# Attention and MLP in one kernel: batches pipelined in a manual order, heads in pairs, 64-key streaming blocks, wide exp and transposes

## The chip, the cores and the metric

The kernel runs on one core of one Trainium2 chip. The metric is device time in microseconds (us), the median of several executions. The executions of one kernel lie 0.1 to 1.5% apart, so I call differences under 2 us of the whole time nothing. Where a change is smaller, I read it from the stages of the profile. Times within a profile are counted from the start of its span, and the span is some 2 us shorter than the measured time.

## The reference

Four batches, 768 tokens, 8 heads of 64. Heads 0, 2 and 6 ("retrieval") have causal attention. The other five ("streaming") see only the first 4 keys (the sinks) and the last 64. The result, 512 wide, goes through an MLP that mixes tokens (768x768, twice) and channels (512x512, twice).

```
scores = q @ k.T / 8;  mask: causal, or causal & (key < 4 or query - key < 64)
x      = softmax(scores) @ v            -> [4, 768, 512]
theta  = x @ w_theta                     # "phases"
zr, zi = x * cos(theta), x * sin(theta)
y      = w_tok_r @ zr + w_tok_i @ zi     # "mixing", over tokens
u      = x + y
out    = u + relu(u @ w_ch)
```

## The kernel before

It is written in program order, attention of all four batches, then the MLP, and a scheduler orders the instructions. The parts that matter here:

```python
# attention, per batch and pair of neighbouring heads, per block of 128 tokens
nc.sync.dma_start(out=tmp..., in_=src[sl])                 # 64 KB
nc.gpsimd.tensor_copy(tmpb, tmp)                           # cast to bf16
nc.tensor.transpose(pt, tmpb, ident)                       # one 128x128
(nc.vector.tensor_copy if si == 0 else nc.scalar.copy)(dst[:, sl], pt)
# ... per head and block j of 128 keys, at most 512 queries
nc.tensor.matmul(ps[:, :cn], kT[:, j*128:(j+1)*128], qT[...], start=True, stop=True)
nc.scalar.activation(at[...], ps[:, :cn], AF.Exp, scale=scale)
# ... per block of queries: mask, then values (65 columns: v and a column of ones)
nc.vector.tensor_tensor(blk, blk, m, ALU.mult)
nc.tensor.matmul(av[i], blk, vt[:, j, :], start=(n == 0), ...)
# ... normalization, per head and block
nc.vector.reciprocal(r, av[i][:, D:D+1])
nc.scalar.activation(xe, av[i][:, :D], AF.Copy, scale=r)
nc.vector.tensor_copy(x_sb[b][i][:, h*D:(h+1)*D], xe)
# [cut] then transposes of x, the token weights (loaded and transposed), and per batch:
# phases (4 matmuls, two sines, two products on DVE), mixing (12 matmuls, add, 4 transposes),
# channels (4 matmuls, relu on ACT, add on DVE, store)
```

The softmax here doesn't subtract the row's maximum and nothing guards it: scores larger than these inputs give would overflow.

## Time and profile before

| | before |
|---|---|
| median | 379.77 us (378.25 to 380.51, 4 runs) |
| span of the profiled run | 377.8 us |
| one batch of attention | 48 us |
| one batch of MLP | 29.4 us (mixing 22.6, phases 6.8) |
| transposes of x, between attention's end and the first mixing | 205 to 246 us |

The prediction shows the lines. Its first fence has busy time by engine and then the span in 40 slices, a digit being tenths of a slice. A timeline row has start, duration, engine, source line, operation, output and inputs, shape and count, and in brackets how long the engine was idle before and what ended that. A matmul's *duration* is modelled and holds its latency, so the cost of a matmul in a stream is the distance from its start to the next one's.

### The profile page before, as it was taken

Reading aid. Unit: us, or ns where it says so; the run is one execution under the profiler, and the core shown is the slowest. Engines: PE = TensorE matmul, PEld = TensorE weight load, DVE = VectorE, ACT = ScalarE, POOL = GpSimd, SP = SyncE. Lnnn points to the kernel's source line nnn. Section 1 sums busy time; section 2 is a strip of 40 time slices with the busy share of each in tenths; the row PEclk is TensorE's granted clock in tenths of the full one; section 3 lists DMA queues with packets and bytes.
Section 4 is the critical chain, followed back from the end, with each engine's and each line's share of the span. In section 5 each row is a group of like instructions: output and inputs, shape, how many; then the busy total and the mean of one; then the engine's idle time right before and its main releaser. Section 6 shows DMA issues by size and latency. Waiting matters only on the chain.

```text
span 377.8 us, 6882 instructions
## 1 busy us (share of the span) xinstructions
PE 313.4 (83%) x1709; PEld 141.5 (37%) x1724; DVE 241.0 (64%) x1243; ACT 197.1 (52%) x598; POOL 97.2 (26%) x406
## 2 busy tenths in 40 slices
PE   0178897889878899789897985687998998999994
PEld 0033443334333434334343443343553443443442
DVE  1126674666756667666576679666788558658655
ACT  1048787877778778777787673000037018008103
POOL 7156545444454445544441000000000000000000
PEclk9999999999999999999999988576999999999999
DMA  6955445444443444434440000034022004004004
GB/s 185 261 129 121 107 92 113 100 95 95 97 100 87 102 110 99 95 88 104 108 102 1 2 0 1 0 90 162 1 84 86 2 0 167 2 1 167 2 0 167
DMA packets 84616, 31.39 MB, mean 83 GB/s; under 512 B 78944, under 2 KB 79968, under 8 KB 84576
## 3 DMA queue, kind: packets, MB, share of 16 engines
q1 hardware_dynamic: 83520, 29.91, 30.3%
q0 software_dynamic: 1056, 1.05, 1.7%
q8 instruction: 13, 0.21, 0.2%
q14 instruction: 27, 0.22, 0.2%
HBM read 25.69 MB, written 6.29 MB: 85 GB/s over the span
## 4 chain that ended last, share of the span: by engine, by line
PE 60%; DVE 14%; ACT 14%; issue 5%; DMA 4%; SPq 1%; POOL 0%; ACTq 0%; POOLq 0%; DVEq 0%
PE ps L136 16%; PE py L215 8%; PE py L212 8%; PE avt L152 8%; ACT at L138 7%; PE pc L225 4%; PE pth L198 4%; PE pt L103 4%; DVE at L151 4%; ACT xe L158 4%; PE pt L165 3%; DVE xT L166 2%; DVE x L159 2%; DMA tmp<-in_q_dram 2%; PE pt L220 2%
## 5 line engine op out<-in xcount | busy, mean ns | idle before, releaser
L138 ACT ACTIVATE at<-ps 128x256 bf16<-128x256 f32 (+3 forms) x236 | 95.4, 420 | 31.8 <-PE avt L152 14.8
L136 PE MATMUL ps<-qT,kT 64*128 64x256 bf16 (+3 forms) x236 | 92.7, 424 | 11.6 <-ACT at L138 5.5
L101 POOL CAST tmpb<-tmp 128x128 bf16<-128x128 f32 x192 | 56.9, 305 | 95.2 <-PE pt L103 27.1
L152 PE MATMUL avt<-vt,at 128*128 128x65 bf16 x552 | 65.1, 243 | 12.3 <-DVE at L151 9.0
L228 ACT ACTIVATE rl<-pc 128x512 f32<-128x512 f32 x24 | 14.3, 597 | 108.5 <-PE pc L225 108.5
L158 ACT ACTIVATE xe<-avt,r 128x64 bf16<-128x64 f32 x192 | 58.4, 313 | 13.5 <-DVE r L156 12.5
L103 PE MATMUL pt<-ident,tmpb 128*128 128x128 bf16 x192 | 49.5, 288 | 19.2 <-POOL tmpb L101 11.6
L152 PEld LDWEIGHTS <-at 128*128 128x128 bf16 x552 | 39.9, 120 | 54.7 <-DVE at L151 41.4
L159 DVE COPY x<-xe 128x64 bf16<-128x64 bf16 x192 | 37.8, 198 | 17.7 <-ACT xe L158 17.1
L103 PEld LDWEIGHTS <-tmpb 128*128 128x128 bf16 x192 | 20.0, 116 | 59.0 <-POOL tmpb L101 31.0
L212 PE MATMUL py<-zr,wrT 128*128 128x512 bf16 x141 | 39.8, 392 | 1.0 <-ACT ct L203 0.8
L215 PE MATMUL py<-zi,wiT 128*128 128x512 bf16 x140 | 39.4, 392 | 0.1
L104 DVE COPY qT<-pt 128x128 bf16<-128x128 bf16 x96 | 20.7, 216 | 25.8 <-PE pt L103 22.2
L156 DVE RECIPROCAL r<-avt 128x1 f32<-128x1 f32 x192 | 28.9, 157 | 11.4 <-PE avt L152 11.4
L104 ACT COPY kT<-pt 128x128 bf16<-128x128 bf16 x96 | 25.3, 265 | 19.7 <-PE pt L103 19.0
L136 PEld LDWEIGHTS <-kT 64*128 64x128 bf16 x236 | 20.8, 103 | 25.6 <-issue 9.2
L198 PE MATMUL pth<-w_theta_sb,xT 128*128 128x512 bf16 x92 | 27.3, 414 | 2.4 <-ACT ct L203 1.6
L151 DVE TENSOR_TENSOR at<-at,m_causal 128x128 bf16<-128x128 bf16 x72 | 16.6, 239 | 17.0 <-ACT at L138 16.4
L165 PE MATMUL pt<-ident,x 128*128 128x128 bf16 x96 | 19.0, 260 | 8.6 <-DVE xT L166 8.4
L217 DVE TENSOR_TENSOR u<-x,py 128x512 bf16<-128x512 bf16 x24 | 16.5, 687 | 14.5 <-PE py L215 13.6
L107 POOL CAST vt<-tmpv 128x64 bf16<-128x64 f32 x96 | 23.4, 244 | 8.9 <-DMA tmpv<-in_v_dram 7.9
L221 DVE COPY uT<-pt 128x128 bf16<-128x128 bf16 x96 | 18.8, 221 | 10.4 <-PE pt L220 9.4
(51 smaller groups left out, 345.8 us busy)
## 6 DMA issues: line engine op xcount, KB each, us to landing
tmp<-in_q_dram SPq DMA_DIRECT2D x96, 64.0 KB, 2.1
tmp<-in_k_dram SPq DMA_DIRECT2D x96, 64.0 KB, 2.1
tmpv<-in_v_dram SPq DMA_DIRECT2D x96, 64.0 KB, 2.2
out_dram<-ot SPq DMA_DIRECT2D x24, 256.0 KB, 2.0
tmp<-in_moe_w_tok_r_dram SPq DMA_DIRECT2D x6, 384.0 KB, 4.4
tmp<-in_moe_w_tok_i_dram SPq DMA_DIRECT2D x6, 384.0 KB, 3.4
w_theta_sb<-in_moe_w_theta_dram POOLq DMA_DIRECT2D x1, 512.0 KB, 6.0
w_ch_sb<-in_moe_w_ch_dram POOLq DMA_DIRECT2D x1, 512.0 KB, 10.1
```

Source lines behind the costliest of these rows:

```text
L101: nc.gpsimd.tensor_copy(tmpb, tmp)
L103: nc.tensor.transpose(pt, tmpb, ident)
L104: (nc.vector.tensor_copy if si == 0 else nc.scalar.copy)(dst[:, sl], pt)
L136: nc.tensor.matmul(ps[:, :cn], kT[:, j * 128:(j + 1) * 128], qT[:, sq0 + off: sq0 + off + cn], start=True, stop=True)
L138: nc.scalar.activation(at[:, sq0 + off:sq0 + off + cn], ps[:, :cn], AF.Exp, scale=scale)
L151: nc.vector.tensor_tensor(blk, blk, m, ALU.mult)
L152: nc.tensor.matmul(av[i], blk, vt[:, j, :], start=(n == 0), stop=(n == len(js) - 1), skip_group_check=True)
L158: nc.scalar.activation(xe, av[i][:, :D], AF.Copy, scale=r)
L159: nc.vector.tensor_copy(x_sb[b][i][:, h * D:(h + 1) * D], xe)
L198: nc.tensor.matmul(pth, xT_sb[b][kk][:, i * 128:(i + 1) * 128], w_theta_sb[:, kk, :], start=(kk == 0), stop=(kk == KD - 1))
L212: nc.tensor.matmul(py, wrT[s][:, t * 128:(t + 1) * 128], zr[s], start=(s == 0), stop=False)
L215: nc.tensor.matmul(py, wiT[s][:, t * 128:(t + 1) * 128], zi[s], start=False, stop=(s == NB - 1))
```

## The change

Its intent: put attention of batch b+1 under the MLP of batch b, in an order fixed by hand, and give each engine fewer and wider instructions. Cut to its core:

```diff
+    ctx.enter_context(tc.manual_schedule())
+PAIRS = [(0, 2), (4, 6), (1, 3), (5, 7)]          # two heads, one in each row half
+            for pair in range(max(map(len, mms))):  # scores: the two heads in turn
+                for y in range(2):
+                        nc.tensor.matmul(o, l, r, start=True, stop=True, ...)
+                # streaming heads: 64 keys against 128 queries, output in a column half
+                            half = slice(64 * (c % 2), 64 * (c % 2) + 64)
+                            mms[y].append((ps[half, y, ...], kT[n][rows, c*64:(c+1)*64], qT[n][rows, lo:hi]))
-                    nc.scalar.activation(at[...], ps[:, :cn], AF.Exp, scale=scale)
+                nc.scalar.activation(P[:, :, :w0], ps[:, :, :w0], AF.Exp, scale=scale)   # two banks
+        # six transposes into one bank, one copy of 768 columns
+                for j in range(NB):
+                    nc.tensor.transpose(pt[:, j*128:(j+1)*128], src[:, j], ident)
+                    nc.scalar.copy(dst[n], pt[:, :S])
+        # normalization of four heads at once, on DVE alone
+            nc.vector.reciprocal(r, av[:, :, D])
+            nc.vector.tensor_tensor(dst, av[:, :, :D], r.unsqueeze(2).to_broadcast([128, 4, D]), ALU.mult)
+            nc.gpsimd.tensor_tensor(zi[:, i], x[:, i], st, ALU.mult)                     # was DVE
+            nc.vector.scalar_tensor_tensor(ot, pc, 0.0, u[:, t], ALU.max, ALU.add)       # relu and add
+    drain(transposes(0)); drain(scores(0)); drain(values(0)); drain(token_weights())
+    for b in range(B):
+        if b + 1 < B:
+            for n in range(4):
+                cast(b + 1, n)
+            weave((phases(b), 5184), (transposes(b + 1), 2720))
+            fetch(b + 1)
+            weave((mix(b), 23000), (chain(scores(b + 1), values(b + 1)), 14000))
+        else:
+            drain(phases(b))
+            drain(mix(b))
```

`weave` advances its parts in proportion to their estimated cost. [Cut: the masks, the sink keys of all streaming heads scored by one set of matmuls, a copy of v shifted by 64 tokens for the half-width value matmuls, and the token weights cast by the transfer itself.]

## The prediction

> **What bounds the kernel now.** I read the page first (busy shares, then slices), then the windows view to split the span, then the chain, the timeline of TensorE, and the groups by shape.
>
> ```profile
> PE 313.4 (83%) x1709; PEld 141.5 (37%) x1724; DVE 241.0 (64%) x1243; ACT 197.1 (52%) x598; POOL 97.2 (26%) x406
> ...
> PE   0178897889878899789897985687998998999994
> PEld 0033443334333434334343443343553443443442
> DVE  1126674666756667666576679666788558658655
> ACT  1048787877778778777787673000037018008103
> POOL 7156545444454445544441000000000000000000
> ```
>
> The reader is to see two programs in a row. ACT and POOL work in the first 22 slices (attention) and almost nothing after (MLP), so adding the stages up engine by engine wastes each engine for half of the time. The windows view puts numbers on it:
>
> ```profile
> core 0: us, PE busy (x) PEld busy (x) DVE busy (x) ACT busy (x) POOL busy (x), PEclk, DMA share, GB/s
> 25.00:205.00 180.00, 156.39 (x914) 68.76 (x913) 117.51 (x809) 140.70 (x486) 85.55 (x356) 1.00 0.43 98
> 205.00:283.00 78.00, 64.80 (x350) 32.85 (x356) 56.82 (x269) 19.84 (x47) 0.00 (x0) 0.82 0.12 39
> 283.00:377.80 94.80, 86.33 (x427) 37.90 (x435) 62.47 (x149) 31.78 (x56) 0.00 (x0) 1.00 0.16 60
> ```
>
> In the attention stage TensorE counts as busy 87% of the time, but its 914 matmuls would fit in far less. The timeline shows why:
>
> ```profile
> 42.43 0.39 PE L136 MATMUL ps<-qT,kT 64*128 64x256 bf16 x1
> 42.76 0.35 PE L152 MATMUL avt<-vt,at 128*128 128x65 bf16 x3
> 43.04 0.39 PE L136 MATMUL ps<-qT,kT 64*128 64x256 bf16 x1
> 43.36 0.29 PE L103 MATMUL pt<-ident,tmpb 128*128 128x128 bf16 x1
> 43.59 0.28 PE L136 MATMUL ps<-qT,kT 64*128 64x128 bf16 x1
> ```
>
> A 64-row score matmul of 256 columns starts at 42.43 and the 128-row one behind it at 42.76: 330 ns later. In the MLP 512 columns take 216 ns start to start, so 256 should take 107. The switch of shape costs some 0.15 to 0.22 us, and the scheduler mixes shapes freely. So the attention stage is bound by many small instructions, with waits passed between TensorE, ACT and DVE. The MLP is bound by matmuls and, between batches, by ACT's sines:
>
> ```profile
> 343.54 0.88 PE pth L198 x4
> 344.44 0.60 ACT st L202
> 345.66 1.04 PE pth L198 x4
> 347.22 0.69 ACT ct L203
> 347.95 1.04 PE pth L198 x4
> ```
>
> From the first matmuls of py and pth in the timeline, one MLP batch takes 29.4 us (320.8 to 350.2): 22.6 of mixing and 6.8 of phases. One attention batch takes 48 us (the last x copies of batches 0, 1, 2 end at 75.8, 123.7, 171.8).
>
> **What the Trainium skill says.** "TensorEngine Tiling (Array Packing)", Key Properties, says that a change of tiling mode drains TensorE; the 330 ns above agree. "ScalarE: Activation LUTs", What ACT_TABLE_LOAD costs, gives 1283 ns for the load; this trace has two, 1283 ns each. "VectorE: DVE Perf Modes", the perf-mode tier table, gives tensor_tensor two elements a cycle in bf16 from SBUF and one from PSUM or in fp32; the trace agrees: a 128x128 bf16 mask is 218 to 239 ns, a 128x512 with PSUM or fp32 684 to 692. "GPSIMD Engine Reference", the comparison of a tensor_tensor on GPSIMD with DVE, has 4497 ns at 2048 fp32 elements. The kernel before has no such operation on POOL; my estimate from that page is 1.2 us for 512 elements.
>
> **The change part by part.** Durations for new sizes are fits to rows of the groups by shape:
>
> ```profile
> L138 ACT ACTIVATE at<-ps 128x256 bf16<-128x256 f32 x124 | 46.3, 384 | 8.0 <-PE ps L136 4.4
> L138 ACT ACTIVATE at<-ps 128x512 bf16<-128x512 f32 x56 | 33.4, 597 | 22.1 <-PE avt L152 14.8 <-PE ps L136 6.4
> L158 ACT ACTIVATE xe<-avt,r 128x64 bf16<-128x64 f32 x192 | 58.4, 313 | 13.5 <-DVE r L156 12.5
> L159 DVE COPY x<-xe 128x64 bf16<-128x64 bf16 x192 | 37.8, 198 | 17.7 <-ACT xe L158 17.1
> ```
>
> An exp grows by 213 ns for 256 columns, 0.83 a column on 171: 1.03 us for 1024. A PSUM copy of 128 columns is 221; at 0.52 ns a column 512 are 0.42 and 768 are 0.55 on DVE (0.8 on ACT).
>
> 1. *Removed:* 236 exps become 56 of mostly 1024 columns; per batch 9 x 1.03 + 3 x 0.6 + 0.92 + 0.39 + 0.7 = 13.1 us against 24.4. All 192 ACT scalings (58.4 us) and 192 DVE copies (37.8) go; 48 wide DVE multiplies of some 0.43 and 48 reciprocals of 0.16 take their place. The 24 ACT relus go into one DVE operation. 372 masks become 72.
>
> 2. *Moved:* the built order on TensorE shows a long start for batch 0, three periods (phases of batch b with transposes of b+1, then mixing of b with scores and values of b+1), and an end with phases and mixing of batch 3.
>
> 3. *The mixing stage, per period, TensorE:* 96 matmuls x 0.216 = 20.7; 48 transposes x 0.056 = 2.7; retrieval scores, two heads in the two row halves at once, 2688 columns / 2.4 = 1.1 and again 1.1 for the third head; 65 streaming score matmuls at an assumed 0.05 = 3.3; sink scores 3 x (0.216 + 0.056) = 0.8; values 88 x 0.054 (spacing of L152 in the timeline) = 4.75 and 60 half-width at 0.05 = 3. Sum 37.5. The order has 54 changes of array shape in the stage; at 0.15 (the low side of the above, as some change only the columns) 8 us. With 1.5 of stalls: 47 us. Beside it ACT has 13.1 + 6 copies x 0.59 + a table load = 17.9, DVE 6 x (0.69 + 0.69) + 12 x 0.59 + 6 x 0.42 + masks 5.9 = 23.8. So TensorE bounds it.
>
> 4. *The phases stage:* TensorE 24 x 0.216 + 48 x 0.056 = 7.9; ACT 6 x (0.684 + 0.598) + 4 x 0.8 + 1.28 for the table = 12.2. POOL now multiplies zi, behind the casts of pairs 2 and 3, which wait for the transposes of pairs 0 and 1 since the cast buffers are two deep; st is two deep as well, so ACT's third sine waits for POOL's first product. From about 5.3 us: 6 x 1.2 = 7.2, plus key-sink copies: 13 to 14.5. I take 14; the next mixing needs zi for its second half. Period 47 + 14 = 61; three are 183.
>
> 5. *The start:* one batch is 18.9 MB / 4 = 4.72 MB. 98 GB/s at a share of 0.43 is 228 GB/s at full share: 21 us, with latency and cast some 25 until the last transpose, and scores come after all transposes. Scores are ACT's: 13.1 + 14 hand-overs = 14.5, to 39.5. POOL, behind the last value casts (28) and selects (30.5), issues 14 weight transfers at 0.8 (752 and 876 ns in the trace) before it copies the key sinks that the sink scores need: 43.5. Values 7.75 + 1.3 + drains 3.6 = 12.7, to 57; twelve token-weight groups at 0.6 (DVE) to 64.5. I take 65.
>
> 6. *The end:* phases 10 (ACT 9), mixing 22 as before, the last transpose, copy, matmuls, add and store 5 (the chain has 1.98 for the store): 37.
>
> Sum 65 + 183 + 37 = 285. I shade it to 280, since the row and column halves may overlap better than 0.05 a matmul.
>
> **Rivals.** (a) *Shape changes cost nothing or are hidden*: each period loses 8, the start 4, and phases run at ACT's 12: some 250. For: transposes tucked between py matmuls cost 55 ns in the trace. Against: the 330 ns above. (b) *The fixed order stalls TensorE*: a hand-written order can't fill a wait, and py, pc and pth share two PSUM buffers, values and transposes two more. Each u addition (0.69) or normalization (0.59) behind a busy DVE would stall TensorE; at 0.3 us for 24 such places 7 per period: about 305. For: the scheduler before filled waits with other work. Against: each buffer is reused only after another group's 0.86 us. (c) *POOL becomes the bound*, were a product 2 us and not 1.2: 5 more in each of four phases, 300. Nothing in the trace speaks to it but the casts, 305 ns for 128 columns. (d) *The start is hidden less*: the weights compete with batch 1's loads; token weights may come 5 to 10 us late: 288.
>
> **Range and chances.** (a) and (b) set the ends: 252 to 306. A gain under 2% would need 90 us of new stalls; that is improbable, though correctness of my reading of buffers leaves a little. Faster 0.97, same 0.02, slower 0.01.
>
> **What would show it right or wrong.** The windows by stage should give first py at 79 us, periods of 61 (phases 14, mixing 47), an end of 37. In the mixing TensorE should be busy over 85% with few waits; a start-to-start of over 0.15 us beyond the columns at each change of shape confirms step 3. Exp at 1024 columns 1.03, POOL's zi 1.2, four waits of ACT for POOL in each phases stage. Wrong: mixing under 41 (drains free), TensorE idle over 15% there naming DVE (rival b), zi over 1.6 (c), or a start beyond 72 naming a transfer (d).

## The result, and the profile after

The changed kernel takes 260.31 us (median, 259.24 to 261.58, 4 runs) against 379.77. Ratios are computed as the mean time of one kernel's fast runs over that of the other's in the same rounds, so they are not quite the ratio of the medians: 0.6848, 95% interval 0.6815 to 0.688. The prediction of 280 (252 to 306) holds, from its fast side.

The page of the changed kernel, busy times and two of the rows of slices:

```profile
PE 202.8 (79%) x1880; PEld 112.1 (44%) x1908; DVE 143.9 (56%) x304; ACT 111.5 (43%) x156; POOL 113.0 (44%) x168
...
PE   1303674998868989989689899886999998869992
...
ACT  1201875000689742026797520266867302551110
```

TensorE's busy time fell by 111 us with 171 more matmuls recorded; ACT has 156 instructions where it had 598. ACT now works in every period, where before it had only bursts once attention had ended. The windows view by stage, cut at the first matmul of phases and at the first of mixing in each batch:

```profile
core 0: us, PE busy (x) PEld busy (x) DVE busy (x) ACT busy (x) POOL busy (x), PEclk, DMA share, GB/s
0.00:25.90 25.90, 5.72 (x46) 4.71 (x47) 7.96 (x19) 3.86 (x5) 19.69 (x42) 1.00 1.00 228
25.90:64.60 38.70, 30.26 (x342) 20.15 (x343) 21.55 (x59) 13.86 (x17) 12.41 (x26) 1.00 1.06 202
64.60:75.70 11.10, 8.22 (x71) 4.92 (x71) 6.91 (x10) 8.12 (x14) 9.65 (x10) 1.00 0.00 0
75.70:116.70 41.00, 37.31 (x386) 19.74 (x391) 26.22 (x61) 19.53 (x26) 15.48 (x25) 1.00 0.57 145
220.80:228.10 7.30, 5.88 (x26) 2.27 (x25) 5.65 (x6) 5.95 (x11) 5.01 (x4) 1.00 0.00 0
228.10:257.40 29.30, 22.91 (x118) 10.26 (x119) 11.25 (x14) 4.73 (x8) 3.98 (x3) 0.99 0.14 54
```

The reader is to see a start of 64.6 us, a period of 11.1 + 41.0 = 52.1 (there are three; the other two are alike but for 1.3 us moved between stages in the third), and an end of 36.6. In the mixing TensorE is busy 37.31 of 41 us. The change of array shape, which the prediction read from the kernel before, looks like this now, in the timeline of TensorE:

```profile
103.71 0.35 PE L298 MATMUL pav<-vt,P 128*128 128x65 bf16 x6
103.99 0.22 PE L305 MATMUL pav<-vx,P 128*64 128x65 bf16 x1
104.00 0.22 PE L306 MATMUL pav<-vt,P 128*64 128x65 bf16 x1
104.15 1.04 PE L356 MATMUL py<-zr,wtokTr 128*128 128x512 bf16 x4
```

The two half-width matmuls start at the same time (103.99 and 104.00): they lie in different column halves. Over the whole stage, taking start to start from the trace: a value matmul of 65 columns behind another comes after 29 to 32 ns (median of 77: 32), a half-width one 0 to 6 ns (median 3) behind its partner in the other column half and the next pair some 32 ns after that, a mixing matmul of 512 columns after 216, and the same followed by a change to 64 rows after 312. A change of shape thus costs 96 ns there. From a full-width value matmul to a half-width one it is 124 ns, 92 more than the median of 32.

The phases stage, as ACT, POOL and DVE see it (rows of three engines' timelines, batch 0):

```profile
69.05 0.74 ACT L326 ACTIVATE ct<-pth,half_pi 128x512 f32<-128x512 f32 x1
71.80 0.60 ACT L327 ACTIVATE st<-pth 128x512 f32<-128x512 f32 x1 [2.01 <-POOL zi L329]
```
```profile
70.17 3.83 POOL L329 TENSOR_TENSOR zi<-x,st 128x512 bf16<-128x512 bf16 x3
```

And three groups by shape (busy, mean of one in ns, then idle time before):

```profile
L218 ACT ACTIVATE P<-ps 128x1024 bf16<-128x1024 f32 x36 | 35.7, 1027 | 11.3 <-PE ps L214 11.2
L329 POOL TENSOR_TENSOR zi<-x,st 128x512 bf16<-128x512 bf16 x24 | 32.1, 1357 | 30.8 <-ACT st L327 30.5
L328 DVE TENSOR_TENSOR zr<-x,ct 128x512 bf16<-128x512 bf16 x24 | 27.2, 1141 | 16.0 <-ACT ct L326 16.0
```

ACT's third sine waits 2.01 us for POOL's first product, as foreseen. What was not foreseen stands in the last row: zr, untouched by the change and 684 ns before, is 1141 now. It shares its time with POOL's zi.

### The profile page after: what moved, and what is told of

It is laid out like the page before. It is cut to its first block, busy times and chain, and to the rows that moved or that the text cites. A ratio compares the mean times of both kernels' runs of the same rounds, so it can differ in the third digit from the quotient of the medians.

```text
span 257.4 us, 4782 instructions
## 1 busy us (share of the span) xinstructions
PE 202.8 (79%) x1880; PEld 112.1 (44%) x1908; DVE 143.9 (56%) x304; ACT 111.5 (43%) x156; POOL 113.0 (44%) x168
## 3 DMA queue, kind: packets, MB, share of 16 engines
q1 hardware_dynamic: 78820, 25.19, 39.7%
## 4 chain that ended last, share of the span: by engine, by line
PE 53%; ACT 11%; DVE 11%; DMA 6%; issue 6%; POOL 6%; SPq 5%; POOLq 0%; DVEq 0%
PE py L356 22%; PE pc L345 7%; PE pav L298 6%; SPq L111 5%; PE ps L214 5%; DMA wtok<-in_moe_w_tok_r_dram 4%; PE pav L305 3%; PE pth L323 3%; DVE zr L328 3%; ACT ct L326 3%; DVE x L268 3%; ACT qT L145 2%; PE pt L339 2%; ACT P L218 2%; POOL zi L329 2%
## 5 line engine op out<-in xcount | busy, mean ns | idle before, releaser
L218 ACT ACTIVATE P<-ps 128x1024 bf16<-128x1024 f32 (+2 forms) x52 | 44.0, 880 | 18.2 <-PE ps L214 18.2
L116 POOL CAST qb<-st_q 128x768 bf16<-128x768 f32 x16 | 14.7, 921 | 73.8 <-issue 52.1
L329 POOL TENSOR_TENSOR zi<-x,st 128x512 bf16<-128x512 bf16 x24 | 32.1, 1357 | 30.8 <-ACT st L327 30.5
L356 PE MATMUL py<-zr,wtokTr 128*128 128x512 bf16 x140 | 38.8, 383 | 4.3 <-DVE zr L328 1.7
L356 PE MATMUL py<-zi,wtokTi 128*128 128x512 bf16 x137 | 36.7, 380 | 0.7 <-issue 0.5
L328 DVE TENSOR_TENSOR zr<-x,ct 128x512 bf16<-128x512 bf16 x24 | 27.2, 1141 | 16.0 <-ACT ct L326 16.0
L326 ACT ACTIVATE ct<-pth,half_pi 128x512 f32<-128x512 f32 x24 | 16.9, 703 | 38.1 <-PE pth L323 38.0
L214 PE MATMUL ps<-qT,kT 64*64 64x128 bf16 (+6 forms) x356 | 27.5, 268 | 6.2 <-ACT P L218 6.0
L214 PEld LDWEIGHTS <-kT 64*64 64x64 bf16 (+1 forms) x356 | 12.5, 112 | 26.7 <-issue 25.1
L345 PE MATMUL pc<-w_ch_sb,uT 128*128 128x512 bf16 x87 | 23.1, 380 | 1.1 <-issue 1.0
L268 DVE TENSOR_TENSOR x<-pav,r 128x256 bf16<-128x256 f32 x48 | 20.4, 425 | 1.7
L347 DVE SCALAR_TENSOR_TENSOR ot<-pc,u 128x512 f32<-128x512 f32 x24 | 16.6, 691 | 5.3 <-PE pc L345 4.1
L143 PEld LDWEIGHTS <-qb 128*128 128x128 bf16 x96 | 7.6, 109 | 27.0 <-issue 13.9
```

The lines of the kernel that those rows point to most:

```text
L143: nc.tensor.transpose(pt[:, j * 128:(j + 1) * 128], src[:, j], ident)
L214: nc.tensor.matmul(o, l, r, start=True, stop=True, skip_group_check=True)
L218: nc.scalar.activation(P[:, :, :w0], ps[:, :, :w0], AF.Exp, scale=scale)
L268: nc.vector.tensor_tensor(dst, av[:, :, :D], r.unsqueeze(2).to_broadcast([128, 4, D]), ALU.mult)
L326: nc.scalar.activation(ct, pth, AF.Sin, bias=half_pi)
L328: nc.vector.tensor_tensor(zr[:, i], x[:, i], ct, ALU.mult)
```

## The experiments

Twelve kernels, all with right results. Each ratio is against the kernel before on the same chip; that of the changed kernel is 0.6848.

| run | median us | ratio | 95% interval |
|---|---|---|---|
| changed kernel | 260.31 | 0.6848 | 0.6815 to 0.688 |
| a1_unwoven | 306.93 | 0.8098 | 0.8041 to 0.8155 |
| a2_zi_on_dve | 255.26 | 0.6726 | 0.6693 to 0.6759 |
| a3_exp_by_bank | 258.36 | 0.6804 | 0.6769 to 0.6838 |
| a4_start_by_pair | 258.6 | 0.6817 | 0.679 to 0.6845 |
| b1_start_by_pair_vs | 253.43 | 0.6661 | 0.661 to 0.6712 |
| b2_heads_not_in_turn | 259.5 | 0.6824 | 0.6792 to 0.6856 |
| b3_narrow_copies | 267.03 | 0.7014 | 0.6971 to 0.7057 |
| b4_stream_128 | 257.9 | 0.6773 | 0.6733 to 0.6813 |
| c1_unwoven_filled | 304.01 | 0.8 | 0.7973 to 0.8026 |
| c2_start_and_dve | 245.6 | 0.6468 | 0.644 to 0.6497 |
| c3_phases_inside | 261.99 | 0.689 | 0.6861 to 0.6919 |
| c4_phases_inside_later | 251.57 | 0.6628 | 0.658 to 0.6676 |

### What is the interleaving worth?

```diff
-            weave((mix(b), 23000), (chain(scores(b + 1), values(b + 1)), 14000))
+            drain(mix(b))
+            drain(chain(scores(b + 1), values(b + 1)))
```

> Scores and values of batch b+1 come after the mixing of batch b and not inside it; all else as in the changed kernel, results right. Theory A (the interleaving hides attention's waits for ACT and DVE under the MLP's matmuls): mixing alone 23 us as in the end stage, scores then bound by ACT at about 14.5 us, values about 13 us as in the start: 50 us in place of 41 in each of the three periods, so 260 + 27 = about 287 us. Theory B (the gain over the kernel before is from fewer and wider instructions alone, and interleaving only adds changes of array shape, 54 against some 30): 260 - 3 x 2.4 = about 253 us.

It took 306.93 us: 47 us of the gain of 119 are the interleaving, and theory B is out. But theory A had asked for 287, so it lacked something too. The windows view of the unwoven kernel, scores, values and phases of one period:

```profile
104.10:118.90 14.80, 9.42 (x95) 5.09 (x96) 6.05 (x18) 11.26 (x14) 0.00 (x0) 0.61 0.34 90
118.90:133.80 14.90, 13.39 (x175) 9.91 (x174) 9.49 (x30) 1.98 (x2) 0.00 (x0) 0.50 0.01 1
133.80:147.70 13.90, 11.36 (x70) 6.69 (x71) 7.37 (x9) 8.93 (x15) 10.68 (x12) 0.75 0.01 1
```

Scores take 14.8 us, bound by ACT as expected (exps are the largest part of the chain in this stage). The column behind POOL's is the granted clock: 0.61, 0.50 and 0.75. Values and phases run at half the clock for much of their time, and the phases take 13.9 us, not 11.1. The Trainium skill, "TensorE: Matmul & The Clock Gate", Part 1, describes this: the clock is halved unless TensorE is busy, and a matmul of N columns then comes every N/1.2 ns and not N/2.4 + 2.5. That makes, by my estimate from these formulas, 54 ns for 65 columns at half the clock and 30 at the full one, and this trace agrees:

```profile
122.57 0.69 PE L298 MATMUL pav<-vt,P 128*128 128x65 bf16 x9
```

Nine value matmuls take 0.69 us with some 0.24 of latency at the end: 56 ns each, where the woven kernel's six in 0.35 (latency 0.21) take 28. The median in this values stage is 54 and in the woven mixing 32.

Some of the 47 us is neither: the three mixings took 28.7, 25.7 and 22.8 us. In each of the first two a channel matmul waits for the output addition on DVE (3.0 and 2.7 us), which itself waits 5.3 and 5.0 us for a store to land. These stores stand in SP's queue behind the loads of the next batch; the third mixing has no loads beside it and no such wait. I did not separate that part by a run.

The next run keeps the clock up by force: unread matmuls of 512 columns, woven into scores and values.

```diff
+            weave((scores(b + 1), 7000), (filler(10, 4), 7000))
+            weave((values(b + 1), 7000), (filler(12, 1), 7000))
```

> The unwoven kernel again (mixing, then scores, then values), with matmuls of 512 columns woven into scores (40) and values (12) whose result nobody reads; results right. Theory A (without the MLP beside it attention is too thin to hold TensorE's clock, and half of what interleaving is worth is the clock): 52 x 0.216 = 11 us more work a period, yet the granted clock stays near 1.0 through scores and values, value matmuls of 65 columns come every 30 ns and not 55, scores plus values 27 us or less in place of 29.6, the phases behind them 11 us and not 13.7: total 306.9 - 3 x 4 = about 294 us. Theory B (the clock is a by-product, attention waits for ACT and DVE): scores plus values 30 us or more, total 307 us or more.

```profile
104.50:120.60 16.10, 15.44 (x133) 6.24 (x136) 5.95 (x18) 11.91 (x14) 0.00 (x0) 1.00 0.31 82
120.60:133.40 12.80, 11.24 (x187) 8.07 (x187) 9.30 (x31) 1.98 (x2) 0.00 (x0) 1.00 0.01 3
133.40:144.40 11.00, 8.17 (x70) 4.94 (x71) 6.75 (x9) 8.19 (x14) 9.72 (x10) 1.00 0.00 0
```

The granted clock stays at 1.00, value matmuls come every 32 ns (median), values are 2.1 us shorter though 12 matmuls were added to them, and the phases are back at 11.0. That settles the mechanism: the same value matmuls come every 54 or 32 ns, by the clock. In total, 304.01 against 306.93 with 34 us of useless matmuls in it; I had expected 294, so the size was off. Over the whole span the three values stages are 6.5 us shorter and the three phases stages 6.0, but the scores are 4.3 us longer with their filler, the mixings 3.2 and the start 1.1. As an estimate, the clock is at least these 12.5 us of the 47 that interleaving is worth, and with the filler of the values (36 x 0.216) up to 20.

### Which part of the change bought something?

zi back on DVE:

```diff
-            nc.gpsimd.tensor_tensor(zi[:, i], x[:, i], st, ALU.mult)
+            nc.vector.tensor_tensor(zi[:, i], x[:, i], st, ALU.mult)
```

> The product zi goes back from POOL to DVE; results right. In the changed kernel zr on DVE took 1.14 us and not 0.69, and zi on POOL 1.36. Theory A (the two engines hold each other up, so the move to POOL freed nothing): zr and zi 0.69 us each where no cast runs beside them, the waits of ACT for zi (2.0 us per phases stage) go, phases 11.1 to about 9.5 us, the end's phases the same 7 us or a little less: total about 255 us. Theory B (the move to POOL relieves DVE): DVE has 6 x 0.69 more in each phases stage and delays the key copies, phases about 13 us, total about 266 us.

255.26 us, theory A: the move to POOL cost 5 us. zi is 684 ns on DVE (median) and zr 693 (1071 in the changed kernel, median). Phases went from 11.1 to 10.8 us, mixing from 41.0 to 40.5, the end from 36.5 to 34.6. The gain is smaller in the phases than expected and larger elsewhere. The Trainium skill, "GPSIMD Engine Reference", Specifications, says that POOL shares its SBUF interfaces with DVE and contends with DVE instructions that have two SBUF inputs. zr is one, and the trace agrees.

Exp in one bank at a time:

```diff
-                nc.scalar.activation(P[:, :, :w0], ps[:, :, :w0], AF.Exp, scale=scale)
+            for y in range(2):
+                nc.scalar.activation(P[:, y, :width[y]], ps[:, y, :width[y]], AF.Exp, scale=scale)
```

> Each exp of two PSUM banks is split into two of one bank; results right. ACT gains 13 instructions a batch at about 0.17 us: 2.2 us. Theory A (ACT bounds the scores of the start only; in the mixing it has 41 us for 20 of work): the start grows by up to 2 us but the key sinks' wait for POOL (2.5 us) hides it, the periods stay at 52.1: 260 to 262 us. Theory B (ACT's latency sets when the score buffers come free in the mixing too): 2 us a period more, about 267 us.

258.36 us, no slower than the changed kernel. The wide exp is worth nothing here: in the mixing ACT has 41 us for 20 of work. Theory A.

Heads not in turn:

```diff
-            for pair in range(max(map(len, mms))):
-                for y in range(2):
-                    if pair < len(mms[y]):
+            for y in range(2):
+                for pair in range(len(mms[y])):
```

> The two heads of a pair are not alternated: all score matmuls of one row half, then all of the other; results right. Theory A (matmuls in different row halves run at the same time: in the changed kernel they start 3 to 4 ns apart): the mixing grows by 1.1 us for the retrieval pair and about 1 for the streaming heads, 43 in place of 41, total about 266 us. Theory B (the pairing gives nothing, weight loads or ACT bound the scores): 260 us as before.

259.5 us, as the changed kernel; but the run does not decide between the theories. Where a bank takes one matmul (four of the six units of the retrieval pair) the edit changes nothing, and elsewhere a quarter or more of the half-array matmuls still start within 7 ns of the one before, in all shapes but one: column halves, or one head's last and the next one's first, still lie side by side. What pairing is worth stays open.

Narrow copies behind the transposes:

```diff
-                    nc.scalar.copy(dst[n], pt[:, :S])
+                    for j in range(NB):
+                        nc.scalar.copy(dst[n][:, j*128:(j+1)*128], pt[:, j*128:(j+1)*128])
 # and likewise for kT, xT, uT and the token weights
```

> The wide copies out of PSUM behind the transposes are cut into copies of 128 columns, as in the kernel before; results right. ACT gains 20 x 0.265 - 4 x 0.28 = some 3 us a phases stage and 2.9 a mixing stage, DVE 3.1 and 2.8, token weights 72 x 0.22 - 12 x 0.57 = 9 us. Theory A (phases are bound by ACT, token weights by DVE): start +9, each phases stage +3: about 279 us. Theory B (only the serial token weights show): about 269 us.

267.03 us, 7 more. The start grew by 3.7 us and the four phases stages by 0.2 to 2.3. So the wide copies are worth some 7 us, less than either theory said: both had added the durations of narrow copies, and copies behind one another overlap (in the kernel before two of 221 ns take 0.36 us).

Streaming heads in blocks of 128 keys:

```diff
+        BAND = [[(0, 0, 256), (1, 128, 256)], [(2, 256, 256), (3, 384, 256)], [(4, 512, 256), (5, 640, 128)]]
-            for w in ((0, 512), (512, 256)):
+            for w in BAND:
                 units.append((n, [(0, h0, w), (1, h1, w)]))
 # masks per piece of 128 queries, whole-width value matmuls, no shifted copy of v
```

> Streaming heads in blocks of 128 keys in place of 64: 11 pieces of scores a head (1408 columns of exp and not 768), masks per piece, whole-width value matmuls, no shifted copy of v; results right. TensorE changes its array shape 26 times a mixing stage and not 54. Theory A (TensorE bounds the mixing, ACT and DVE have room): halves cost 1.7 us of matmul now, 3.2 then, and 28 changes at 0.1 us go: 1.4 us a period less; the start has 3.2 us more of exp: total 256 to 260 us, so the 64-key blocks are worth nothing. Theory B (exp and masks matter in the mixing): ACT +3.2 and DVE +6 us show, 3 us a period: about 271 us.

257.9 us: no slower, and theory A. The first mixing went from 41.0 to 38.2 us: nearly twice as many exp columns of the streaming heads, and more masks, fit beside TensorE, and half of the shape changes are gone. The phases stage lost 1.6 us of that again, with a granted clock of 0.87 there, and the start 2.1. The 64-key blocks, the most intricate part of the change, bought nothing.

Of the gain of 119 us these runs place 47 in the interleaving and 7 in the wide copies. Some 65 no run takes apart: the order fixed by hand in place of the scheduler's, the wide normalization, the fewer and larger loads, and the stretch between attention's end and the first mixing, which took 41 us before and takes 18 in the changed kernel's first batch (57.3 to 75.8 us).

### What binds the start?

Batch 0's scores follow its transposes pair by pair, and the weights' transfers are issued behind the key sinks:

```diff
-    drain(transposes(0))
-    drain(scores(0))
+    tg, sg = transposes(0), scores(0)
+    for units in (6, 4, 2, 2):
+        next(tg); next(tg)
+        for _ in range(units):
+            next(sg)
+    drain(tg)
+    # [moved here: the 14 weight transfers issued by POOL]
+    drain(sg)
```

> Batch 0's scores follow its transposes pair by pair, and the weights' transfers are issued by POOL behind the key-sink copies and not ahead of them; results right. Theory A (the start is bound by the order: scores wait for the last pair's load, and the sinks for POOL's weight transfers): scores end at about 30 us and not 38.7, values at 43 and not 57, token weights at about 52 where their transfers then bind: total about 248 us. Theory B (the start is bound by the transfers alone): token weights still end at 60 or later, total over 256 us.

258.6 us, nothing gained, and for a reason that neither theory named:

```profile
23.34 1.04 PE L214 MATMUL ps<-qT,kT 64*128 64x512 bf16 x4 [15.43 <-DVE kT L147]
```

The first score matmul waited 15 us for the first key copy on DVE. Ahead of that copy in DVE's queue stood the copy of the sink values, which waited for a transfer queued behind all loads of batch 0:

```profile
21.98 0.83 DVE L410 CAST vs<-vs_f 128x1280 bf16<-128x1280 f32 x1 [11.77 <-DMA vs_f<-in_v_dram]
```

DVE took its instructions in the order of the program, so one early instruction that waited 11.77 us held the key copy (22.75 us) behind it. The next run moves the sink copy as well.

```diff
+    # [moved behind the scores: tensor_copy(vs, vs_f), the ones and POOL's selects on them]
```

> As the earlier run with the start by pairs, in which DVE stood until 23 us: in its queue the copy of the sink values, which waits for a transfer behind all loads of batch 0, lay ahead of the first key copy. Here that copy and POOL's selects on it come behind the scores too; results right. Theory A (the start is bound by the order): first scores at about 9 us, scores end at 30, values at 43, token weights at about 52: total about 248 us. Theory B (loads and weight transfers bind): token weights end at 60 or later and the total stays over 256 us.

253.43 us. Scores now begin at 10.7 us and the last x is transposed at 44.4, as theory A said, but the first phases matmul is at 58.1: POOL issued the first weight transfer only at 34.2 us, behind selects that waited 2.9 us for the moved copy and ended at 31.9 (the 2.3 us after them the profile gives to no wait). Last, the selects early, the transfers right behind the key sinks, and zi on DVE:

> Start by pairs with the weights' transfers issued right behind the last key-sink copy (selects on the sink values made early, so POOL need not wait for them), and zi on DVE; results right. In the last such run the transfers began at 34 us and bound token weights to 58. Theory A: transfers begin at 27 us, last about 23, token weights end at 51: start 13 us shorter than the changed kernel's 64.7, periods 51.3 as with zi on DVE: total 253.2 + 2 - 13 = about 242 us. Theory B (loads of batch 1 on the same engines stretch the transfers): start 58 or later, total 248 us or more.

245.6 us, the fastest of all. The transfers begin at 29.9 us and phases at 54.7. Its ratio over the changed kernel's is 0.6468/0.6848 = 0.944. It missed 242: the transfers began 3 us later than expected, so the start was 3 us longer, and two of the periods took 52.0 and 52.4 us and not 51.3.

### Can phases go inside the mixing too?

```diff
+    def attend(b):                       # woven with mix(b - 1)
+        yield from scores(b)
+        for k, cost in enumerate(values(b)):
+            yield cost
+            if k in (4, 7, 10, 13, 16, 17):
+                yield next(pg)           # one phase of batch b
+            elif k:
+                yield next(tg, 1)        # one transpose group of batch b + 1
 # zr and zi twice, sines in bf16
```

> As the run before it, and the phases of batch b+1 and the transposes of batch b+2 go inside the mixing of batch b too, behind each value group; zr and zi twice, sines in bf16 to make room; results right within the tolerance. Theory A (TensorE bounds the whole period once ACT's sines lie beside matmuls): 41 us of mixing + 8 us of TensorE work of phases and transposes = 47 to 49 us a period in place of 51.3, and batch 3's phases (7 us) leave the end: total 242 - 9 - 7 = about 226 us. Theory B (three users of two PSUM buffers and of ACT in order stall TensorE): periods 51 us or more, total about 235 us or more.

261.99 us, 16 more than c2_start_and_dve, with first mixing matmuls 58.2, 57.1 and 51.5 us apart: theory B. The longest of TensorE's waits, in the list of waits (total, times, longest), and that row again after the phases were put two value groups later:

```profile
PE pth L324 <- DVE xT L274: 14.0, 13, 2.4
```
```profile
PE pth L324 <- DVE xT L274: 4.2, 3, 1.8
```

```diff
-            if k in (4, 7, 10, 13, 16, 17):
+            if k in (6, 9, 12, 15, 17):
```

> The run before it with phases inside, which took periods of 51.5 to 58 us, TensorE waiting 14 us in all for the x copies on DVE since each phase stood right behind the transposes of its own x. Here each phase comes two value groups later; results right within the tolerance. Theory A (those waits are what it lost): the waits of pth for DVE go under 3 us in all, periods 50 to 53 us, total 245 to 250 us, no better than the version with the start by pairs and zi on DVE. Theory B (the loss is elsewhere: more changes of array shape, DVE as a second bound): the waits go but the total stays over 255 us.

The median of 251.57 us and the ratio in the table are over all four runs, of which two (254.46 and 252.87) are slow, at a granted clock of 0.97. The two fast ones, 248.71 and 250.26, have a mean of 249.5 (a ratio of 0.657): inside theory A, though two of the three periods (54.4 and 52.9 us) are not. Those waits were 10 of the 16 us lost, and the time fell by 12 between fast runs. It is still 4 us slower than c2_start_and_dve. The waits of score matmuls for exps are 8.2 us in all here and 4.7 there, which is about that size; no run tests it.

## Why the prediction was right, point by point

**The bound.** Right: TensorE bounds the mixing (busy 37.3 of 41 us), ACT and DVE have room, which the runs with more exp and more masks confirm.

**The start** was predicted at 65 us and took 64.6. Its steps ended where they should: last transposes 25 (26.0), scores 39.5 (38.7), sinks free of POOL 43.5 (42.9 for the last sink matmul), values 57 (57.3), token weights 64.5 (64.5). Inside the POOL step this was luck. POOL began to issue at 26.3 us and not 30.5, an issue took 0.53 to 0.58 us (0.93 and 0.75 for the two large ones) and not 0.8, and what filled the time was a wait: after eight transfers POOL stood for 3.66 us until the first had landed, then some 0.6 before each further one. In the trace the ninth transfer waits on the semaphore that the first one raises: the program gives these transfers eight semaphores in turn.

```profile
34.64 0.54 POOL L421 DMA_DIRECT2D wtok<-in_moe_w_tok_i_dram  x1 [3.66 <-DMA w_theta_sb<-in_moe_w_theta_dram]
```

**The end**, 37 us, took 36.5.

**The mixing** was predicted at 47 us and took 41.0 (39.7 in the last period), just where the prediction would have called itself wrong ("mixing under 41"); this is the main mis-sized term, three times. Item by item, measured against predicted: values 88 x 0.03 = 2.6 us and not 4.75; half-width values 0.7 and not 3; streaming scores 1.0 and not 3.3; 54 changes at 0.1 = 5.4 and not 8. That is 9 us less, of which 3 came back: 41.0 less these and the unchanged items leaves 4.9 us for stalls and not 1.5, and the list of waits for this stage has 3.4 of them. The failing words are "values 88 x 0.054 (spacing of L152 in the timeline)". That 54 ns is 65 columns at half the clock. The change of shape was read from the same stretch, and wrongly: the 107 ns taken off the 330 for the columns came from the MLP at full clock. In the attention, a value matmul comes 218, 324, 429 and 536 ns (medians) after a score matmul of 128, 256, 384 and 512 columns, so a column costs 0.83 ns there and not 0.42, and a change some 112 ns and not 220. The sign that was to confirm this step, over 0.15 us a change, failed with it. The kernel before thus ran its attention at half the clock by this reading, while the windows view gives 1.00 there. The trace holds no clock record before 219.9 us of that span, and where there is none the view shows full clock; the changed kernel's start, before its first record at 59.0 us, has 55 ns too. That the kernel before was slow there for this reason I infer from these spacings; for the changed kernel's code, the unwoven and the filled run show it. Interleaving therefore gave more than overlap: it held the clock. None of my parts had that.

The two assumed 0.05 us were wrong for another reason: matmuls in different halves of the array start 3 to 4 ns apart.

**The phases** were predicted at 14 us and took 11.1. POOL's product was 1.36 us (mean) and not 1.2, so that term erred the other way, but the stage did not last until the last product: the first mixing matmul starts at 75.8 us with zr alone, and POOL's last two products follow it (76.6 to 79.4). ACT waited for POOL once in the first stage (2.0 us) and not four times, and 5 times, 6.6 us, in the four stages. The contention that the move created (zr at 1141 ns) was missed.

**Rivals.** (a) was half right: the changes cost two thirds of what I took, not nothing. (b) did not come: over the whole span TensorE waits 1.6 us for u and 3.1 for x. It did in c3_phases_inside, for xT. (c) was small as put (its 300 counts 20 us from 280, where (b) counts from the sum, 285), but the product on POOL did cost 5 us (a2_zi_on_dve). (d) did not come. A slip without effect: of masks the trace has 68 and not 72.

**Range and chances.** The shading to 280 was too timid: the low end, 252, assumed free changes, and the truth came near it by cheaper matmuls instead; that the range held is in part luck.

## What to carry to other kernels

Read a matmul's cost from start to start, and ask at which clock the stretch that you read it from ran: 65 columns every 54 ns say half. Thin stages of TensorE are worth putting inside dense ones twice over, for the overlap and for the clock. In a manual order look at each queue's first waiting instruction: here one sink copy, then the selects behind it, held the start by 10 us, and that was worth more than 64-key blocks and wide exps together.

## What the Trainium skill lacked or had wrong

- "TensorE: Matmul & The Clock Gate", Part 1, ties the half clock to an idle window of about 3.4 us (and, further on, to short gaps between bursts, without a measure). In a1_unwoven the clock fell, or stayed low, in stages whose longest wait of TensorE was 0.9 us: scores with 9.4 of 14.8 us recorded busy went to 0.61, values with 13.4 of 14.9 to 0.50. With 40 matmuls of 512 columns added to the scores and 12 to the values it stayed at 1.00.
- "TensorEngine Tiling (Array Packing)", Key Properties, says that a change of mode drains TensorE, but not what that costs: 92 to 96 ns at full clock (124 less 32 ns, 312 less 216), 120 at half (174 less 54, in a1_unwoven's values).
- "GPSIMD Engine Reference", Specifications, names the contention with two-input DVE instructions without a size (other pages of the skill say more of it, and are not compared here): zr on DVE 684 ns alone and 1141 (mean) beside POOL's product, which took 1.15 us at best and 1.36 on average. My estimate from that page's 4497 ns was 1.2.
